# Batch 0's tokens in quarters, a held weight load and paired transposes in an attention and MLP kernel

## The chip, the cores and the metric

The kernel runs on one core of one Trainium2 chip. The metric is device time in microseconds (us) of one execution; the number compared is the median of several runs. Times inside an execution come from the hardware profiler, counted from the start of its span.

## The reference

`x` is (8, 8, 512, 64): batch, head, token, feature. `state` is (8, 8, 32, 64). All inputs are float32.

```
scores  = 1/8 * x @ state^T                # per batch and head: 512 x 32
a       = softmax(scores, over the 32)     # max taken off, 1e-9 added to the sum
xread   = a @ state                        # 512 x 64
scores2 = 1/8 * state @ x^T                # 32 x 512
a2      = softmax(scores2, over the 512)
sread   = a2 @ x                           # 32 x 64
y       = concat([xread, sread], tokens)   # 544 rows per head
rows    = y with the heads side by side    # (8 * 544) x 512
out     = leaky_relu(rows @ w_in, 0.01) @ w_out    # w_in 512 x 2048, w_out 2048 x 512
```

## The kernel before, in words

The instruction order on every engine is written out by hand. The tile pools decide only where buffers lie; waits follow from the data.

**The algebra.** For the 512 token rows of a batch, `xread @ w_in` is computed as `a @ (state @ w_in)`. `a_m` (matmuls on L384) makes a piece of `M = state @ w_in` for one 512-column chunk of w_in, `m_evict` (L396, L398) casts it to SBUF, and `ff1` (L405, for batch 0 `ff1_0` on L632) multiplies it with the transposed probabilities `aT`. `piece` (L433) is the second product with w_out, in four quarters `jq` of the sum for each of four row blocks `i`. The 256 state rows of all batches go through the MLP at the end (`ff1_s`).

**Start.** SP issues the transfers of batch 0's tokens (tiles `xf`), ACT that of the first states (`st0f`). GpSimd (POOL) makes an identity and small masks, and then issues in order the loads of w_in (four chunks of 512 columns, cast to bf16 by the DMA), w_out, batch 1's tokens (`x1`) and batch 2's (`xl`). TensorE (PE) first runs `spin` matmuls on zeros, seven of them, then `state01` (transposed states, tile `stbd`), then three more.

**Batch 0.** Two halves `u` of four heads. `cast_x0` casts tokens to bf16, PE transposes them (`x0_half`, L487), `xt0_evict` copies them from PSUM (L494), `scores0` makes the scores with tokens on the partitions (L502, tiles `sct`), `max0` takes maxima (L531), `split0` splits each into two bf16 parts, `rows0` computes the scores again with states on the partitions (L514), and `spread0` adds the maxima to them by matmuls (L523). `exp0`, `sum0`, `recip0`, `recip0_rows` and `probs0` finish the softmax (L544 to L567). Then come `a_m` of chunks 0 and 1, the first four `ff1_0` blocks, and `a_m` of chunk 2, which needs w_in's third load.

**Batches 2 to 7.** A loop over batches with 16 slots `s`. Every slot holds one `ff1` block of the batch and one `piece`; between them stand steps of the next batches: token load (s = 0), scores and maxima (s = 1), exponentials (s = 5 to 7), `a_m` (s = 10), a DMA transpose of the tokens after next (s = 13).

**Second probabilities.** `a_probs2` writes `a2` (states on the partitions). A DMA transpose from SP makes `a2T`, and `a_sread` (PE L357, ACT copies on L364) reads it for `sread`. Batches 0 and 1, and batches 6 and 7, share a tile `a2p` and are transposed in one DMA (`a_a2t_pair`); batches 2 to 5 have one DMA each (`a_a2t`, L339), issued at s = 0 behind the token load (L99), with `a_sread` at s = 8 of the same batch. `a_sread` of batches 0 and 1 stands at s = 4 and 6 of batch 2, that of batch 6 at s = 6 of batch 7.

Of the kernel before, what the change touches and what calls it, by code (L numbers as in the profile page):

```python
# [9 lines left out]
P = 128  # L10
B, H, S, D = 8, 8, 512, 64
NS = 32
# [3 lines left out]
NT = S // P  # L16
NK = H // 2
SCALE = 1.0 / (D ** 0.5)

BF16 = mybir.dt.bfloat16  # L20
FP32 = mybir.dt.float32
# [6 lines left out]
def kernel(  # L28
# [9 lines left out]
    nc = tc.nc  # L38

    consts = ctx.enter_context(tc.tile_pool(name="consts", bufs=1))  # L40
# [18 lines left out]
    nc.scalar.dma_start(  # L59
        st0f[:], state[0:2].rearrange("b h n d -> (b h n) d").rearrange("(p r) d -> p r d", r=4)  # L60
    )
    xf = [consts.tile([P, NK, 2 * P], FP32, name="xf", tag=f"xf{u}") for u in range(2)]
    xv = x[0].rearrange("h (p t) d -> p h (t d)", t=NT)
    for u in range(2):
        nc.sync.dma_start(xf[u][:], xv[:, NK * u:NK * (u + 1)])

    idle = consts.tile([P, S], BF16, name="idle")
    nc.vector.memset(idle[:], 0.0)
    warm = consts.tile([P, 2], FP32, name="warm")
# [2 lines left out]
    ident = consts.tile([P, P], BF16, name="ident")  # L72
# [47 lines left out]
    def pair_of(a, t, k):  # L120
        h = 2 * (k % 2)
        return a.xb[k // 2][:, t, h:h + 2, :].rearrange("p h d -> p (h d)")
# [11 lines left out]
            xl[b][:].rearrange("p h (t d) -> p h t d", t=NT),  # L134
        )

    def cast_x0(h0, h1, copy):
        u = h0 // NK
        copy(
            xs[0][u][:, :, h0 - NK * u:h1 - NK * u].rearrange("p t h d -> p h t d"),  # L140
            xf[u][:, h0 - NK * u:h1 - NK * u].rearrange("p h (t d) -> p h t d", t=NT),
        )

    def load_w_in(c):
        nc.gpsimd.dma_start(  # L145
            w_in_bf[:, :, DM * c:DM * (c + 1)],
            moe_w_in[:, DM * c:DM * (c + 1)].rearrange("(k p) f -> p k f", p=P),
        )

    def load_w_out(c):  # L150
        nc.gpsimd.dma_start(
            w_out_bf[:, 4 * c:4 * (c + 1), :],
            moe_w_out[DM * c:DM * (c + 1), :].rearrange("(j p) f -> p j f", p=P),
        )

    def spin(n, tag):
        p = psum.tile([P, S], FP32, name="pspin", tag=tag, bufs=2 if tag in ("ph", "py") else 1)
        for _ in range(n):
            nc.tensor.matmul(p[:], lhsT=idle[:, :P], rhs=idle[:], start=True, stop=True)
# [102 lines left out]
    def block_sub(flat, m1, n):  # L262
        m1b = att.tile([P, n, NS], FP32, name="mrowb", tag="mrowb", bufs=1)
        nc.vector.transpose(m1b[:], m1[:, :, None].to_broadcast([P, n, NS]))  # L264
        sh = att.tile([P, n * NS], FP32, name="sh", tag="sh")
        nc.vector.tensor_tensor(  # L266
            out=sh[:], in0=flat, in1=m1b[:].rearrange("p c j -> p (c j)"), op=ALU.subtract,
        )
        return sh
# [51 lines left out]
    def a_probs2(a):  # L321
        nc.vector.tensor_scalar(out=a.r2[:], in0=a.r2[:], scalar1=1e-9, scalar2=None, op0=ALU.add)
        q2 = att.tile([P, 2], FP32, name="qc", tag="qc")
        nc.vector.reciprocal(q2[:], a.r2[:])
        if a.b in (0, 6):
            pairs[a.b] = att.tile([P, 2, 2, S], BF16, name="a2p", tag="a2p", bufs=1)
        if a.b in (0, 1, 6, 7):
            a.a2 = pairs[a.b - a.b % 2][:, a.b % 2]
        else:
            a.a2 = att.tile([P, 2, S], BF16, name="a2", tag="a2", bufs=1)[:]  # L330
        for g in range(2):
            nc.vector.tensor_scalar(
                out=a.a2[:, g, :], in0=a.e2[:, g, :],
                scalar1=q2[:, g:g + 1], scalar2=None, op0=ALU.mult,
            )

    def a_a2t(a):
        t = att.tile([P, 2, NT, P], BF16, name="a2T", tag="a2T", bufs=1)
        nc.sync.dma_start_transpose(  # L339
            t[:].rearrange("p g i q -> p (g i) q"), a.a2.rearrange("p g s -> p (g s)")  # L340
        )
        a.a2T = t[:]

    def a_a2t_pair(b):
        t = att.tile([P, 2, 2, NT, P], BF16, name="a2pT", tag="a2pT", bufs=1)
        nc.sync.dma_start_transpose(
            t[:].rearrange("p b g i q -> p (b g i) q"),
            pairs[b][:].rearrange("p b g s -> p (b g s)"),
        )
        for v in range(2):  # L350
            att_of[b + v].a2T = t[:, v]
# [125 lines left out]
    VEC(stb0[:], st0f[:])  # L477
    spin(7, "py")
    state01()
    spin(3, "py")  # L480

    def x0_half(u):
        pxt = [psum.tile([P, NT, P], BF16, name="pxth", tag=("ph", "py")[u]) for _ in range(2)]
        for v in range(2):
            for t in range(NT):
                h = NK * u + 2 * v
                nc.tensor.transpose(  # L487
                    pxt[v][:, t, :], pair_of(a0, t, h // 2), ident[:]
                )
        return pxt  # L490

    def xt0_evict(u, pxt, copies):
        for v, copy in enumerate(copies):
            copy(a0.xT[:, :, 2 * u + v, :], pxt[v][:])  # L494

    sct = [psum.tile([P, NG, NS], FP32, name="sct", tag=tag, bufs=1) for tag in ("sc", "big")]

    def scores0(u):
        for v in range(2):
            for t in range(NT):  # L500
                c = NK * t + 2 * v
                nc.tensor.matmul(  # L502
                    sct[u][:, c:c + 2, :].rearrange("p c n -> p (c n)"),
                    lhsT=a0.xT[:, t, 2 * u + v, :],
                    rhs=stbd[:, 2 * u + v].rearrange("p g n -> p (g n)"),
                    start=True, stop=True,
                )

    scn, e10, r0, qb0 = {}, {}, {}, {}

# [55 lines left out]
    def probs0(u):  # L566
        nc.vector.tensor_tensor(out=a0.aT[:, u], in0=e10[u][:], in1=qb0[u][:], op=ALU.mult)  # L567

    load_w_in(0)
    load_w_in(1)  # L570
    cast_x0(0, 2, VEC)
    cast_x0(2, 4, SCA)
    pxt = x0_half(0)
    xt0_evict(0, pxt, (VEC, SCA))
    cast_x0(4, 6, VEC)
    for c in range(2, 4):
        load_w_in(c)
    cast_x0(6, 8, POO)
    load_w_out(0)
    x1 = [consts.tile([P, NK, 2 * P], FP32, name="x1", tag=f"x1{u}") for u in range(2)]  # L580
    for u in range(2):
        nc.gpsimd.dma_start(
# [6 lines left out]
    a0.aT = att.tile([P, 2, S], BF16, name="aT", tag="aT")  # L589
    open_xb(1)  # L590
    a_open(a1, 1)
    scores0(0)
    pxt = x0_half(1)
    m = max0(0)
    xt0_evict(1, pxt, (SCA, VEC))
    rows0(0)
    m = split0(m)
    scores0(1)
    m = m, max0(1)
    rows0(1)  # L600
    spread0(scn[0], m[0], False)
# [153 lines left out]
    for b in range(2, B):  # L755
        hT = hpool.tile([P, 16, S], BF16, name="hT", tag="hT")
        a = att_of[b]
        nxt = att_of[b + 1] if b + 1 < B else None
        order = [(b - 1, i, 3) for i in range(2)]
        order += [(b - 1, i, jq) for i in range(2, NT) for jq in range(4)]  # L760
        order += [(b, i, jq) for jq in range(3) for i in range(2)]
        for s in range(16):
            ff1(a, hT, s)
            if s == 0:
                if b + 2 < B:
                    load_x(b + 2, nc.sync)
                    open_xb(b + 2)
                if b == 7:
                    a_a2t_pair(6)
                elif b != 6:  # L770
                    a_a2t(a)
            elif s == 1:
                if nxt is not None:
                    a_scores(nxt)
                m_evict(a, 3, a_m(a, 3, "big"), SCA)
                if nxt is not None:
                    a_shift(nxt)
                    a_max2(nxt)
                if b + 2 < B:
                    cast_all(b + 2)  # L780
            elif s == 4:
                if b == 2:
                    load_state(1)
                    a_sread(a0)
            elif s == 6:
                if b in (2, 7):
                    a_sread(a1 if b == 2 else att_of[6])
            elif s == 8:
                if b != 6:
                    a_sread(a)  # L790
                if b == 2:
                    state_cast(1)
                    state_t(1)
            if nxt is not None:
                if s == 5:
                    a_exp(nxt)
                elif s in (6, 7):
                    a_exp2(nxt, s - 6)
                    if s == 7:
                        a_probs(nxt)  # L800
                        a_probs2(nxt)
                elif s == 10:
                    pm0 = a_m(nxt, 0, "big")
                    pm2 = a_m(nxt, 2, "phpy")
                    pm1 = a_m(nxt, 1, "sc")
                    m_evict(nxt, 2, pm2, VEC)
                    m_evict(nxt, 0, pm0, VEC)
                    m_evict(nxt, 1, pm1, SCA)
                if s == 13 and b + 2 < B:
                    a_open(att_of[b + 2], b + 2)  # L810
                    a_xt_dma(att_of[b + 2])
            pb, i, jq = order[s]
            piece(pb, hT if pb == b else h_prev, i, jq)
        h_prev = hT
# [48 lines left out]
```

## Time and profile before

| | |
|---|---|
| median of 3 runs | 216.64 us (216.63 to 217.03) |
| the profiled execution's own time | 216.83 us |
| its span | 214.4 us |
| PE busy | 207.1 us, 97% of the span |
| ACT / DVE / POOL busy | 137.8 / 99.4 / 23.2 us |
| HBM read / written | 17.30 / 8.91 MB |

Busy times are sums over the span, so 97% says that PE is the engine to look at, not that every microsecond of it is needed: the spin matmuls count as busy too. Some matmul records are missing from the trace, so a gap on PE of about one matmul may be a record that was lost. An engine's wait is put down to the semaphore that came last. A DMA has two times: how long its issue keeps the issuing queue, and how long after the issue the data have landed.

### The profile page before, as it was taken

To read this page: it belongs to the slowest core of one execution; us is meant where nothing else is said; L and a number is where in the kernel's file an instruction comes from. 1 tells how busy PE (TensorE), PEld (TensorE's weight loads), DVE (VectorE), ACT (ScalarE), POOL (GpSimd) and SP (SyncE) were. 2 spreads that over 40 slices of the span, in tenths; PEclk is the share of its full clock that TensorE was granted. 3 is DMA by queue.
4 is the path that set the end of the run, shared out by engine and by line. 5 is a ranking of instruction groups with operands and counts; after the bars stand their busy time and mean duration, and the time that the engine had idled before them with its cause. 6 is when DMAs were issued, how large, how long until landed. Compare 5 with 4: busy or idle time off the path is not lost.

```text
span 214.4 us, 3689 instructions
## 1 busy us (share of the span) xinstructions
PE 207.1 (97%) x1482; PEld 97.4 (45%) x1508; DVE 99.4 (46%) x152; ACT 137.8 (64%) x261; POOL 23.2 (11%) x38
## 2 busy tenths in 40 slices
PE   7889999999999999999999999999999999999993
PEld 2533534344454444444454445444444455466553
DVE  1668598699857246741784096706680000000000
ACT  3468567988788476856696579647774756464420
POOL 8831001030031012000200030000000000000000
PEclk9999999999999999999999999999999999999998
DMA  6999995685994991189217931422124210111123
GB/s 174 226 206 293 208 279 116 165 278 88 222 254 119 141 252 67 52 173 232 84 52 150 228 117 49 101 46 101 49 68 79 73 73 3 49 52 49 49 52 98
DMA packets 39872, 27.70 MB, mean 129 GB/s; under 512 B 24496, under 2 KB 35120, under 8 KB 39856
## 3 DMA queue, kind: packets, MB, share of 16 engines
q1 hardware_dynamic: 34912, 21.04, 39.8%
q0 software_dynamic: 4800, 6.29, 14.5%
q10 hardware_dynamic: 144, 0.13, 0.5%
q8 instruction: 12, 0.20, 0.4%
q14 instruction: 4, 0.03, 0.1%
HBM read 17.30 MB, written 8.91 MB: 122 GB/s over the span
## 4 chain that ended last, share of the span: by engine, by line
PE 87%; DMA 5%; DVE 3%; POOL 2%; issue 1%; ACT 1%; POOLq 0%; ACTq 0%
PE py L433 48%; PE ph L405 21%; DMA w_in_bf<-in_moe_w_in_dram 5%; PE pm L384 4%; PE ph L416 3%; PE pyw L433 3%; PE ph L632 2%; PE psr L357 2%; PE pyh L459 2%; PE sc L246 1%; POOL w_in_bf L145 1%; DVE mrow L256 1%; DVE mrowb L264 1%; DVE M L398 1%; DVE sh L266 1%
## 5 line engine op out<-in xcount | busy, mean ns | idle before, releaser
L433 PE MATMUL py<-w_out_bf,hT 128*128 128x512 bf16 x444 | 116.4, 379 | 1.0
L410 ACT ACTIVATE hT<-ph 128x512 bf16<-128x512 f32 x112 | 66.4, 601 | 40.0 <-PE ph L405 39.4
L433 PEld LDWEIGHTS <-hT 128*128 128x128 bf16 x496 | 46.7, 98 | 57.0 <-issue 5.3
L405 PE MATMUL ph<-aT,M 128*128 128x512 bf16 x223 | 65.3, 379 | 0.2
L405 PEld LDWEIGHTS <-M 128*128 128x128 bf16 x224 | 21.7, 98 | 27.3 <-issue 1.9
L442 ACT COPY ysb<-py 128x512 f32<-128x512 f32 x31 | 18.2, 586 | 10.7 <-PE py L433 10.7
L256 DVE TRANSPOSE_TENSOR_REDUCE mrow<-sc 128x32 f32<-128x1024 f32 x7 | 8.7, 1250 | 32.6 <-PE sc L246 32.6
L464 DVE COPY ysh<-pyh 128x256 f32<-128x256 f32 x1 | 0.4, 424 | 48.2 <-PE pyh L459 48.2
L132 POOL CAST xb<-xl 128x2048 bf16<-128x2048 f32 x5 | 9.5, 1894 | 77.4 <-DMA xl<-in_x_dram 44.7
L398 ACT CAST M<-pm 128x1024 bf16<-128x1024 f32 x13 | 13.2, 1013 | 1.2 <-PE pm L384 0.6
L278 DVE TRANSPOSE_TENSOR_REDUCE r<-e 128x32 f32<-128x1024 bf16 x7 | 8.7, 1242 | 10.1 <-ACT e L273 10.1
L398 DVE CAST M<-pm 128x1024 bf16<-128x1024 f32 x9 | 11.0, 1218 | 1.8 <-PE pm L384 1.8
L314 ACT ACTIVATE e<-sc,mcols 128x512 bf16<-128x512 f32 x16 | 11.2, 701 | 0.3 <-DVE mcols L308 0.3
L396 DVE CAST M<-pm 128x512 bf16<-128x512 f32 x12 | 7.7, 685 | 5.4 <-PE pm L384 5.4
L306 DVE TENSOR_REDUCE mcol<-sc 128x2 f32<-128x1024 f32 x8 | 9.7, 1214 | 0.0
L420 ACT ACTIVATE hs<-ph 128x256 bf16<-128x256 f32 x16 | 6.0, 385 | 4.6 <-PE ph L416 4.4
L287 DVE STREAM_TRANSPOSE qb<-qh 128x1024 bf16<-128x1024 bf16 x7 | 8.7, 1246 | 0.2
L264 DVE STREAM_TRANSPOSE mrowb<-mrow 128x1024 f32<-128x1024 f32 x7 | 8.7, 1245 | 0.2
L266 DVE TENSOR_TENSOR sh<-sc,mrowb 128x1024 f32<-128x1024 f32 x7 | 8.6, 1225 | 0.2
L416 PE MATMUL ph<-sr_t,w_in_bf 128*128 128x256 bf16 x64 | 8.3, 273 | 0.0
L640 ACT ACTIVATE hT<-ph 128x512 bf16<-128x512 f32 x12 | 6.4, 597 | 2.4 <-PE ph L632 2.1
L273 ACT ACTIVATE e<-sh 128x1024 bf16<-128x1024 f32 x7 | 7.3, 1050 | 0.6 <-DVE sh L266 0.6
(98 smaller groups left out, 155.0 us busy)
## 6 DMA issues: line engine op xcount, KB each, us to landing
out_dram<-ysb SPq DMA_DIRECT2D x31, 256.0 KB, 2.4
xl<-in_x_dram SPq DMA_DIRECT2D x5, 1024.0 KB, 7.3
w_in_bf<-in_moe_w_in_dram POOLq DMA_DIRECT2D x4, 512.0 KB, 9.4
w_out_bf<-in_moe_w_out_dram POOLq DMA_DIRECT2D x4, 512.0 KB, 16.7
xf<-in_x_dram SPq DMA_DIRECT2D x2, 512.0 KB, 5.1
x<-in_x_dram POOLq DMA_DIRECT2D x2, 512.0 KB, 13.6
xl<-in_x_dram POOLq DMA_DIRECT2D x2, 512.0 KB, 17.1
out_dram<-ysb SPq DMA_DIRECT2D x8, 64.0 KB, 1.7
```

Of the source, the lines that this page charges most:

```text
L132: nc.gpsimd.tensor_copy(xt[b][:].rearrange("p t h d -> p h t d"), xl[b][:].rearrange("p h (t d) -> p h t d", t=NT),)
L256: nc.vector.tensor_reduce(out=m1[:], in_=flat.rearrange("p (c j) -> p c j", j=NS), axis=AX.X, op=ALU.max, apply_transpose=True,)
L264: nc.vector.transpose(m1b[:], m1[:, :, None].to_broadcast([P, n, NS]))
L266: nc.vector.tensor_tensor(out=sh[:], in0=flat, in1=m1b[:].rearrange("p c j -> p (c j)"), op=ALU.subtract,)
L306: nc.vector.tensor_reduce(out=m2[:], in_=a.sc[:], axis=AX.X, op=ALU.max, negate=True)
L314: nc.scalar.activation(out=a.e2[:, g], in_=a.sc[:, g, :], func=AF.Exp, bias=a.m2s[:, g:g + 1], scale=SCALE, accum_out=a.r2[:, g:g + 1],)
L398: copy(a.M[:, :, cols], pm[:])
L405: nc.tensor.matmul(ph[:], lhsT=a.M[:, g, P * j:P * (j + 1)], rhs=a.aT[:, g, :], start=(g == 0), stop=(g == 1),)
L410: nc.scalar.activation(out=hT[:, j, :], in_=ph[:], func=AF.Prelu, alpha=0.01)
L416: nc.tensor.matmul(ph[:, :n], lhsT=w_in_bf[:, k, P * j:P * (j + 1)], rhs=sr_t[:, k, :], start=(k == 0), stop=(k == NK - 1),)
L433: nc.tensor.matmul(y.py, lhsT=hT[:, j, P * i:P * (i + 1)], rhs=w_out_bf[:, j, :], start=(j == 0), stop=(j == 15),)
L442: copy(ysb[:], ys[b, i].py)
```

## The change

- Batch 0's tokens come in four transfers of two heads each, in place of two of four heads. The casts go by quarters: the first on GpSimd, the other three on VectorE (before: VectorE, ScalarE, VectorE, GpSimd).
- GpSimd sets a tile `held` (128 x 640 bf16) to zero before it issues w_in's first load. Its cast of quarter 0 stands between w_in's first and second loads.
- Transposes, copies and scores go by quarters. Three quarters are transposed before any is scored; ScalarE copies the first three, VectorE the last, ahead of the first maximum. The three `spin` matmuls after `state01` are gone.
- Second probabilities of batches (2, 3) and (4, 5) are transposed in pairs too, at s = 0 of the odd batch. `a_sread` of an even batch moves to s = 6 of the batch after it. `a2p` gets two buffers, `sh` one in place of two.

```diff
-    for u in range(2):
-        nc.sync.dma_start(xf[u][:], xv[:, NK * u:NK * (u + 1)])
+    for q in range(NK):
+        nc.sync.dma_start(xf[q][:], xv[:, 2 * q:2 * q + 2])
+    held = consts.tile([P, 640], BF16, name="held")
...
-        sh = att.tile([P, n * NS], FP32, name="sh", tag="sh")
+        sh = att.tile([P, n * NS], FP32, name="sh", tag="sh", bufs=1)
...
-        if a.b in (0, 6):
-            pairs[a.b] = att.tile([P, 2, 2, S], BF16, name="a2p", tag="a2p", bufs=1)
-        if a.b in (0, 1, 6, 7):
-            a.a2 = pairs[a.b - a.b % 2][:, a.b % 2]
-        else:
-            a.a2 = att.tile([P, 2, S], BF16, name="a2", tag="a2", bufs=1)[:]
+        if a.b % 2 == 0:
+            pairs[a.b] = att.tile([P, 2, 2, S], BF16, name="a2p", tag="a2p")
+        a.a2 = pairs[a.b - a.b % 2][:, a.b % 2]
...
     state01()
-    spin(3, "py")
+    def x0_t(q):
+        ps = psum.tile([P, NT, P], BF16, name="pxth", tag=("ph", "py")[q // 2])
+        for t in range(NT):
+            nc.tensor.transpose(ps[:, t, :], pair_of(a0, t, q), ident[:])
+        return ps
...
+    nc.gpsimd.memset(held[:], 0.0)
     load_w_in(0)
-    load_w_in(1)
-    cast_x0(0, 2, VEC)
-    cast_x0(2, 4, SCA)
-    pxt = x0_half(0)
-    xt0_evict(0, pxt, (VEC, SCA))
-    cast_x0(4, 6, VEC)
-    for c in range(2, 4):
+    cast_x0(0, POO)
+    for q in range(1, NK):
+        cast_x0(q, VEC)
+    for c in range(1, 4):
         load_w_in(c)
-    cast_x0(6, 8, POO)
     load_w_out(0)
+    pxt = [x0_t(q) for q in range(3)]
+    for q, copy in ((0, SCA), (1, SCA), (2, SCA)):
+        xt0_evict(q, pxt[q], copy)
+    for q in range(2):
+        scores0(q)
+    xt0_evict(3, x0_t(3), VEC)
...
-    scores0(0)
-    pxt = x0_half(1)
     m = max0(0)
-    xt0_evict(1, pxt, (SCA, VEC))
     rows0(0)
     m = split0(m)
-    scores0(1)
+    for q in (2, 3):
+        scores0(q)
...
-                if b == 7:
-                    a_a2t_pair(6)
-                elif b != 6:
-                    a_a2t(a)
+                if b % 2:
+                    a_a2t_pair(b - 1)
...
             elif s == 6:
-                if b in (2, 7):
-                    a_sread(a1 if b == 2 else att_of[6])
+                if b == 2 or b % 2:
+                    a_sread(att_of[b - 1])
             elif s == 8:
-                if b != 6:
+                if b % 2:
                     a_sread(a)
```

More of the change, by code (lines that the diff above doesn't have):

```diff
@@ L61 @@
     )
-    xf = [consts.tile([P, NK, 2 * P], FP32, name="xf", tag=f"xf{u}") for u in range(2)]
+    xf = [consts.tile([P, 2, 2 * P], FP32, name="xf", tag=f"xf{q}") for q in range(NK)]
     xv = x[0].rearrange("h (p t) d -> p h (t d)", t=NT)
-    for u in range(2):
-        nc.sync.dma_start(xf[u][:], xv[:, NK * u:NK * (u + 1)])
+    for q in range(NK):
+        nc.sync.dma_start(xf[q][:], xv[:, 2 * q:2 * q + 2])
+    held = consts.tile([P, 640], BF16, name="held")
     idle = consts.tile([P, S], BF16, name="idle")
@@ L135, in cast_all, with cast_x0 @@
         )
-    def cast_x0(h0, h1, copy):
-        u = h0 // NK
+    def cast_x0(q, copy):
+        v = q % 2
         copy(
-            xs[0][u][:, :, h0 - NK * u:h1 - NK * u].rearrange("p t h d -> p h t d"),
-            xf[u][:, h0 - NK * u:h1 - NK * u].rearrange("p h (t d) -> p h t d", t=NT),
+            xs[0][q // 2][:, :, 2 * v:2 * v + 2].rearrange("p t h d -> p h t d"),
+            xf[q][:].rearrange("p h (t d) -> p h t d", t=NT),
         )
@@ L335, in a_probs2 @@
             )
[L337 to L342, printed above, removed]
     def a_a2t_pair(b):
@@ L479, with xt0_evict, scores0 @@
     state01()
-    spin(3, "py")
[L482 to L494, printed above, removed]
-    sct = [psum.tile([P, NG, NS], FP32, name="sct", tag=tag, bufs=1) for tag in ("sc", "big")]
[L498 to L507, printed above, removed]
+    def x0_t(q):
[3 more added lines that the diff above has]
+        return ps
+    def xt0_evict(q, ps, copy):
+        copy(a0.xT[:, :, q, :], ps[:])
+    sct = [psum.tile([P, NG, NS], FP32, name="sct", tag=tag, bufs=1) for tag in ("sc", "big")]
+    def scores0(q):
+        for t in range(NT):
+            c = NK * t + 2 * (q % 2)
+            nc.tensor.matmul(
+                sct[q // 2][:, c:c + 2, :].rearrange("p c n -> p (c n)"),
+                lhsT=a0.xT[:, t, q, :], rhs=stbd[:, q].rearrange("p g n -> p (g n)"),
+                start=True, stop=True,
+            )
     scn, e10, r0, qb0 = {}, {}, {}, {}
```

## The prediction

> **What bounds the kernel now.** I read the page first, then PE's waits, the chain of waits, the timeline of the first 32 us and the stretches of the DMA queues. The page:
>
> ```profile
> span 214.4 us, 3689 instructions
> PE 207.1 (97%) x1482; PEld 97.4 (45%) x1508; DVE 99.4 (46%) x152; ACT 137.8 (64%) x261; POOL 23.2 (11%) x38
> ...
> PEclk9999999999999999999999999999999999999998
> DMA  6999995685994991189217931422124210111123
> ```
>
> TensorE is the bound, and the DMA engines are full over the first six slices (32 us). PE's waits from 15.3 us to the end:
>
> ```profile
> PE pm L384 <- DMA w_in_bf<-in_moe_w_in_dram: 0.2, 1, 0.2
> ```
>
> That is the whole list, and it is the wait that has just ended at 15.23. From there on PE never idles long enough to be listed: gaps of one matmul's length (0.43 us between starts where 0.216 is usual) are missing records, 1482 matmuls against 1508 weight loads. So only what happens before 15.23, or a new stall, can move the end. What sets 15.23 is in the chain of waits (start, length, what) and in the timeline:
>
> ```profile
> 4.50 10.69 DMA w_in_bf<-in_moe_w_in_dram
> 15.23 0.63 PE pm L384 x16
> ```
>
> ```profile
> 6.98 0.79 POOL L139 CAST xb<-xf 128x512 bf16<-128x512 f32 x1 [0.87 <-DMA xf<-in_x_dram]
> ...
> 7.50 0.69 DVE L531 TENSOR_REDUCE m<-sct 128x16 f32<-128x512 f32 x1 [0.20 <-PE sct L502]
> ...
> 8.26 0.42 DVE L494 COPY xT<-pxth 128x512 bf16<-128x512 bf16 x1
> ...
> 9.07 0.69 DVE L531 TENSOR_REDUCE m<-sct 128x16 f32<-128x512 f32 x1
> ...
> 13.09 0.39 PE L632 MATMUL ph<-aT,M 128*128 128x512 bf16 x1
> ...
> 15.23 0.41 PE L384 MATMUL pm<-w_in_bf,stbd 64*32 64x512 bf16 x8 [0.24 <-DMA w_in_bf<-in_moe_w_in_dram]
> ```
>
> Two paths meet at 15.23: batch 0's attention, which lets PE begin real work at 13.09 and reaches this point with 0.24 us to spare, and the third chunk of w_in, which lands at 4.50 + 10.69 = 15.19. The second path ends last. It meets PE again later: of the waits up to 45 us,
>
> ```profile
> PEld L246 <- DMA st_t<-stb: 0.5, 1, 0.5
> ```
>
> is batch 2's scores at 40.15, waiting for a transposed state that landed at 36.94 + 3.2 = 40.1 (PE itself loses 0.05: 0.14 between starts where 0.09 is usual). That hangs on batch 2's tokens, loaded behind all the weights (issued 15.47, landed 17.6 later). The DMA path thus holds PE at two places, and the change takes no bytes off it. The stretches of the DMA queues (last column GB/s):
>
> ```profile
> 5.50:6.00 0.50, 0.33 (x4) 0.13 (x4) 0.32 (x1) 0.50 (x1) 0.50 (x1) 1.00 1.10 344
> 6.00:6.25 0.25, 0.25 (x7) 0.25 (x6) 0.00 (x0) 0.00 (x1) 0.12 (x1) 1.00 1.22 250
> ...
> 7.00:8.00 1.00, 0.84 (x14) 0.58 (x12) 0.80 (x2) 0.33 (x2) 1.00 (x2) 1.00 1.22 204
> ```
>
> Batch 0's tokens move at 340 to 390 GB/s from 3.0 to about 6.1, then the casting w_in loads at 204 (bytes written), with no gap. w_in's first load, issued at 2.84, moves next to nothing before 6.0.
>
> **The change part by part.**
>
> *Four transfers.* The halves landed at 0.75 + 4.6 = 5.36 and 1.27 + 5.6 = 6.85, 1.49 apart: 0.745 a quarter, so quarters at 4.6, 5.35, 6.1 and 6.85. Two more SP issues (0.47 each) end near 2.6, ahead of any need. The last may land up to 0.3 earlier if w_in no longer shares 6.0 to 6.5, or no earlier; I take 6.85, since the stream before it is already full.
>
> *The hold.* POOL's memsets took 0.20 us for 128 and 0.26 for 196 columns, 0.9 ns a column; 640 columns give about 0.65 (0.5 by a slope of 0.6 from the 32-row memsets). w_in's first issue moves from 2.84 to 3.45. If its data were ready and queued when x0 ended, this costs nothing; if the 3.1 us from issue to first data (2.84 to about 6.0) are all latency, data start at 6.6 and the queue stands still for 0.45. Nearest rows: 64 KB stores landed 1.7 us after issue in all, and the state loads issued at 23.89 into a full queue took 4.5; so most of a long delay is queueing. I take 0 and keep 0.45. The other three w_in loads move behind the POOL cast, from 3.72 to about 5.5; w_in's first load lands at 9.31, which covers them by some 3 us. Token and weight loads behind them issue 0.3 later (7.72 to 8.0) and wait in the queue until 17.63 anyway.
>
> On sharing, the Trainium skill ("DMA: Bandwidth & Descriptors", Queues, rings and completion order) says that a DMA engine alternates between the queues that have work, packet by packet. By that rule w_in would slow x0 as soon as it is ready and the hold would win that time back; this trace shows x0 at 344 GB/s up to 6.0, so there is little to win back, and by the rule the sum below would be at most 0.3 lower on the attention path, which is not the path that ends last.
>
> *Batch 0's chain.* Quarter 0: POOL cast 0.79 from 4.7 (POOL started 0.13 after landing at 6.98) to 5.5; four transposes to the copy's start 0.49 (cast end 5.82 to copy 6.31): 6.0; three ACT copies of 0.59: 6.6, 7.2, 7.75. Scores of quarter 1 at 7.2; then quarter 3's transposes, whose DVE cast (0.43 from 6.87) is done at 7.30; DVE copy 7.8 to 8.2. Here DVE is in order, so the first maximum, which ran at 7.50 while DVE waited for POOL's cast, now stands behind that copy: 8.2 to 8.9, split 0.4 to 9.3 (8.97 before), second maximum 0.69 to 10.0 (9.76), split to 10.4 (10.18). So the chain gets 0.2 longer: it loses POOL's 0.79 for DVE's 0.43, and gains one 0.69 maximum in series. Real work starts at 13.3, and PE comes to the w_in wait at 15.2 instead of 14.99. The 0.24 of cover just hides it: between 0 and 0.05 on the end, 0.1 to 0.4 if copies or POOL run later than counted. The dropped three spin matmuls (4.76 to 5.70) freed nothing that was waited for.
>
> *Pairs.* Batches 2 and 4 lose their own transposes (SP busy 3.2 and 2.5 us), 3 and 5 issue double ones behind a 1 MB token load, and batch 2's and 4's state reads (16 matmuls, 0.47 us, two ACT copies of 0.26) move into slot 6 of the next batch. PE's work is the same. Cover for the doubled transpose in batch 3: issued at 73.1, the single one landed 7.5 later at 80.6, 0.9 after its token load (72.42 + 7.3); twice the blocks add about 0.9: 81.5. The read now starts two slots before the old one (87.53 less 2 x 1.295 = 84.94): 3.4 to spare. In batch 5: 125.1 against 130.4. The upper bound, twice 7.5 from issue, gives 88.1 and a 3.2 stall. ACT's two copies beside the exponentials are what batch 2 already has at slots 4, 6 and 8, where PE shows no wait. One buffer for sh: its reader is done at 31.83, its next writer starts near 43. SP's stores wait up to 0.8 longer behind the longer issue, with four output buffers to cover. All of this: 0.
>
> *Sum.* The profiled execution took 216.83 (214.4 span and 2.43 around it), 0.19 over the median. Quarters and hold 0, chain +0.2 of which 0.04 to 0.05 passes the w_in wait, pairs 0: 216.9 for such an execution, 216.7 against the median.
>
> **The rivals.**
>
> *The hold starves the queue (0.15).* If w_in's first data come 3.1 us after issue whatever the queue, all landings slip 0.45, with both DMA waits of PE: 217.1. It decides once the hold exceeds the time that w_in's descriptors lay ready before 6.1. For it: data started just as x0 ended. Against it: the 1.7 us of small stores.
>
> *TensorE's clock falls back (0.10).* The first seven spins took 3.17 us, 0.45 each, the next three 0.94, later 512-column matmuls 0.216: the array doubles its speed near 5.0, although the granted clock reads 1.00 throughout. Without the three spins PE works, by the timeline's rows, an estimated 1.5 of the 3.4 us after 4.9 (before: 2.3). If that lets it fall back, the spreads, rows, sums and products between 5.5 and 13.1 take twice their time, some 1.5 us on the path, of which the cover takes 0.04: 218.1. Against it: at 50% busy from 10.3 to 13.1 it stays fast. The Trainium skill ("TensorE: Matmul & The Clock Gate", The HAM clock gate) has the clock halved after an idle window of about 3.4 us; by that rule the scattered work would hold it, unless transposes don't count as work, as its part on PE-mode transposes says. No run here shows which.
>
> *A chain or transpose longer than counted (0.11).* ACT's serial copies or w_in slipping ahead of quarter 3 add 0.5 to 0.8: 217.3; a stalled state read (0.03 of it) up to 220.
>
> *Faster (0.12).* w_in's landings are 2.51, 3.37 and 2.44 apart; were the third even, all later loads would land 0.87 sooner and both DMA waits vanish. With quarter 3 landing 0.3 sooner and scores hidden as they land, the chain could be 0.3 shorter: 0.24 + 0.3 gives 216.1.
>
> **How the numbers follow.** The forecast case has 0.52 and runs from 216.3 to 217.05. Within 0.2% (0.43 us, about what a measurement of this kernel can tell) is that case: 0.52. Slower is the first three rivals, 0.36; faster 0.12. The range reaches to the third rival and takes part of the faster one: 216.2 to 217.7, leaving out the clock and the far ends.
>
> **What would show it.** Right: quarters landing near 4.6, 5.4, 6.1, 6.85; the first ff1 matmul (L632's line) near 13.3; the a_m matmuls behind it still at 15.2 to 15.3, released by w_in; PE without waits in batches 3 and 5. Wrong: a stretch near 6.3 with low GB/s and w_in's third chunk past 15.5 (first rival); 512-column matmuls 0.4 apart between 9 and 13 (second); the wait before a_m gone and PE there before 15.0 (faster).

## The result and the profile after

The changed kernel took 218.24 us in the median of six executions (217.40 to 219.30), the kernel before 216.79 beside it (216.63 to 217.03): a ratio of 1.0072, 95% interval [1.0055, 1.0089]. It is slower, and its median lies above the predicted range. Its profiled execution is its shortest, 217.40 with a span of 215.3, so what follows here explains 0.9 us of span and no more; the rest needs the experiments. The six spans are 215.3 to 216.3; of what lies outside the span (2.10 to 2.16 us in four of the six) two executions have 0.7 and 0.9 us more, and no profile shows what that is. All ratios leave out the two executions that were over 1.5% slower than the fastest of their kernel (220.22 of the quarters alone, 220.81 with w_in's second load ahead of the cast).

The page of the changed kernel:

```profile
span 215.3 us, 3679 instructions
...
PE 206.2 (96%) x1479; PEld 97.2 (45%) x1505; DVE 99.2 (46%) x152; ACT 137.9 (64%) x261; POOL 23.6 (11%) x39
...
PEclk9999999999999999999999999999999999999999
DMA  6999994775884992184217931332024110111113
```

PE is busy for 0.9 us less because the three spin matmuls that are gone took 0.94; the span is 0.9 longer because PE waits. PE's waits from 15.3 us to the end (total, times, longest):

```profile
PE pm L375 <- DMA w_in_bf<-in_moe_w_in_dram: 1.1, 1, 1.1
PE py L424 <- issue: 0.3, 2, 0.2
PE ph L396 <- ACT hT L401: 0.2, 1, 0.2
```

The first is the wait that was 0.2 before; the second are two gaps of 0.16 us for which the profile shows no other engine; the third is taken up with the pairs. The chain of waits shows what set it, and the timeline where batch 0's attention stood (start, length, what):

```profile
2.95 0.64 POOL held L553
3.59 0.82 POOL w_in_bf L146
4.41 0.00 issue
4.41 0.62 POOL xb L140
5.03 0.80 POOL w_in_bf L146
5.83 10.05 DMA w_in_bf<-in_moe_w_in_dram
```

```profile
12.96 0.39 PE L617 MATMUL ph<-aT,M 128*128 128x512 bf16 x1
...
15.93 0.41 PE L375 MATMUL pm<-w_in_bf,stbd 64*32 64x512 bf16 x8 [1.07 <-DMA w_in_bf<-in_moe_w_in_dram]
```

The chain now runs through the memset of `held` and the cast on GpSimd into the third w_in load, which lands at 5.83 + 10.05, at 15.89, instead of 15.19. The attention chain is 0.13 earlier than before (first `ff1_0` matmul 12.96, not 13.09) and buys nothing. The stretches of the DMA queues (last column GB/s):

```profile
5.50:6.00 0.50, 0.45 (x5) 0.23 (x4) 0.17 (x2) 0.41 (x1) 0.50 (x2) 1.00 0.96 184
6.00:6.25 0.25, 0.00 (x0) 0.00 (x0) 0.25 (x1) 0.25 (x2) 0.25 (x1) 1.00 1.01 127
...
7.00:8.00 1.00, 0.99 (x15) 0.57 (x15) 0.55 (x2) 0.36 (x1) 1.00 (x2) 1.00 1.23 194
```

Before, the same stretches moved 344, 250 and 204. The tokens end sooner, and w_in does not follow at its rate: behind the tokens the queues move less (127 GB/s).

**Reading all profiles with one rule.** A point that every profile has is ACT's sixth copy of batch 0's hidden layer (L627 in the changed kernel). In the fifteen profiles of the experiments, and in the two of before and after, it starts at the later of two times: w_in's third landing + 2.54, or the first `ff1_0` matmul + 4.33, to within 0.02 us. So each kernel's front is read from two numbers, and each loss is put to the weights or to the attention chain.

| profile of | w_in's third chunk lands | first `ff1_0` matmul | sixth copy | set by |
|---|---|---|---|---|
| before | 15.19 | 13.09 | 17.73 | w_in |
| changed | 15.89 | 12.96 | 18.43 | w_in |
| changed, again | 16.43 | 14.27 | 18.97 | w_in |
| hold doubled | 17.33 | 15.19 | 19.87 | w_in |
| changed front, pairs undone | 15.65 | 13.99 | 18.32 | chain |
| before, quarters only | 16.70 | 16.89 | 21.21 | chain |
| before, without the three spins | 14.87 | 15.37 | 19.70 | chain |
| changed, without the hold | 15.07 | 16.40 | 20.72 | chain |

From here to PE's last matmul the profiles differ by another -0.3 to +0.5, nearly all of it before 53 us (batch 2's state and first copies).

### The profile page after: what moved, and what is told of

The parts are those of the page before. It is cut to its first block, busy times and chain, and to the rows that moved or that the text cites. A ratio compares the mean times of both kernels' runs of the same rounds, so it can differ in the third digit from the quotient of the medians.

```text
span 215.3 us, 3679 instructions
## 1 busy us (share of the span) xinstructions
PE 206.2 (96%) x1479; PEld 97.2 (45%) x1505; DVE 99.2 (46%) x152; ACT 137.9 (64%) x261; POOL 23.6 (11%) x39
## 4 chain that ended last, share of the span: by engine, by line
PE 85%; DMA 5%; DVE 3%; POOL 2%; issue 1%; ACT 1%; SPq 1%; POOLq 0%; ACTq 0%
PE py L424 49%; PE ph L396 21%; DMA w_in_bf<-in_moe_w_in_dram 5%; PE pm L375 4%; PE ph L407 3%; PE pyw L424 3%; PE ph L617 2%; PE psr L348 2%; PE sc L247 1%; POOL w_in_bf L146 1%; DMA out_dram<-ysb 1%; DVE mrow L257 1%; DVE mrowb L265 1%; DVE mcols L309 1%; DVE M L389 1%
## 5 line engine op out<-in xcount | busy, mean ns | idle before, releaser
L396 PE MATMUL ph<-aT,M 128*128 128x512 bf16 x219 | 64.5, 379 | 0.3 <-ACT hT L401 0.2
L375 PE MATMUL pm<-w_in_bf,st_t 64*32 64x512 bf16 x192 | 7.6, 379 | 0.1
```

The lines of the kernel that those rows point to most:

```text
L375: nc.tensor.matmul(at[v][NS * r:NS * (r + 1)], lhsT=st_of(a, g, k), rhs=w_in_bf[D * g:D * (g + 1), k, DM * c:DM * (c + 1)], start=True, st ...
L396: nc.tensor.matmul(ph[:], lhsT=a.M[:, g, P * j:P * (j + 1)], rhs=a.aT[:, g, :], start=(g == 0), stop=(g == 1),)
```

## The experiments

The ratios are to the kernel before, measured beside each on the same chip, with 95% intervals; medians of before were 216.74 to 216.82.

### The parts by themselves: hold out, pairs alone, hold alone, front alone

The changed kernel without the memset:

```diff
-    nc.gpsimd.memset(held[:], 0.0)
     load_w_in(0)
```

> The changed kernel without the memset of the held tile; all else as changed. Theory H (the hold, together with tokens that now start 0.38 us sooner, lets the DMA queue run thin between 5.7 and 6.5 us): w_in's first load is issued at 2.84 again, its third lands 0.6 to 1.0 us sooner than the 15.89 of the changed kernel, near 15.0, PE's wait before that product falls from 1.07 to under 0.3 us, and the median comes to 216.3 to 216.8, at or below the kernel before. Rival O (the queue runs thin because w_in's second to fourth loads wait behind GpSimd's cast): the third still lands at 15.6 or later and the median stays above 217.2. Rival P (the paired transposes cost most of it): less than 0.3 us gained, median above 217.7.

Measured: 216.86 (216.59 to 219.46), ratio 1.0012 [0.9991, 1.0034]. Taking out one memset brings the median back to that of before, so in this kernel the median's loss goes with the hold. The third chunk lands at 15.07, as theory H expected; the third load is issued at 5.81, as late as in the changed kernel (5.83), so its place behind the cast (rival O) is not what delays it there. But the profile is from the longest execution, 219.46, and shows the other side. w_in's first data came at 5.25, into the tokens' last quarter, which landed at 8.51 instead of 6.51. PE waited 2.5 us for casts, and from 8.2 to 15.0 the granted clock read 0.50: 128-column matmuls took 0.31 each instead of 0.22, and `ff1_0` began at 16.40.

The kernel before with only the second probabilities in pairs (`a2p`, `a_a2t_pair` and `a_sread` as in the change, `sh` with one buffer):

```diff
-                if b == 7:
-                    a_a2t_pair(6)
-                elif b != 6:
-                    a_a2t(a)
+                if b % 2:
+                    a_a2t_pair(b - 1)
```

> The kernel before with only the paired second probabilities (the tiles' buffers, the pair transposes in batches 3 and 5, the moved state reads). Theory H: no change, 216.6 to 217.0, PE without waits in batches 3 and 5. Rival P: 0.6 to 1.4 us slower than before, with PE waits after 48 us.

Measured: 217.19 (216.66 to 217.64), ratio 1.0014 [1.0004, 1.0024], 0.2 above the range of theory H and below that of rival P. PE's waits from 15 us to the end in this kernel:

```profile
PE py L423 <- issue: 0.3, 2, 0.2
PE ph L395 <- ACT hT L400: 0.3, 1, 0.3
PE pm L374 <- DMA w_in_bf<-in_moe_w_in_dram: 0.2, 1, 0.2
```

None of it is a wait for a transposed tile. From ACT's 29th to its 124th copy of the hidden layer (52 to 185 us) this kernel takes 133.63 us, the kernel before 133.63, the changed one 133.64. The 0.3 on `hT` stands near 48 us, where ACT's exponentials waited 0.50 for `mcols` instead of 0.28. It is not the pairs' own: the changed kernel has it in its first profile (0.2 above) and not in its second, and two kernels without the pairs have it (0.2 with three token transfers, 0.7 with four on two queues). So the pairs cost nothing in the steady state; where the 0.1 to 0.5 us of the ratio lie, this profile does not show.

The kernel before with only a hold (two memsets of 300 columns, which move the first issue from 2.84 to 3.65):

```diff
+    held = consts.tile([P, 300], BF16, name="held")
+    for _ in range(2):
+        nc.gpsimd.memset(held[:], 0.0)
     load_w_in(0)
     load_w_in(1)
```

> The kernel before with two memsets of 300 columns ahead of w_in's first load (0.6 us of hold), tokens still in halves. Theory H: in the changed kernel the data came 2.1 us after the issue, so here they are ready near 5.6, before the halves end at 6.15: 0 to 0.2 us slower than before. If the 3.1 us from issue to data in the kernel before were all latency: 0.5 to 0.6 us slower, data from 6.6.

Measured: 217.19 (216.77 to 217.42), ratio 1.0013 [1.0004, 1.0023]. The third chunk landed at 15.48, 0.29 later, and PE ended 0.15 later. With w_in's loads issued in one go behind the hold, the 0.8 us by which they are issued later cost 0.3 at the landing and, by the ratio, 0.1 to 0.5 in time; half a microsecond is hidden.

The changed kernel with its pairs undone (front, hold and `sh` as changed):

```diff
-                if b % 2:
-                    a_a2t_pair(b - 1)
+                if b == 7:
+                    a_a2t_pair(6)
+                elif b != 6:
+                    a_a2t(a)
```

> The changed kernel with the second probabilities of batches 2 to 5 transposed singly as before (sh keeps one buffer). Theory H: as the changed kernel, 217.4 to 218.5, third w_in load near 15.9. Rival P: back to within 0.3 us of the kernel before.

Measured: 218.15 (217.41 to 219.12), ratio 1.0060 [1.0038, 1.0082]: the loss is in the front. In this profile w_in's third chunk lands at 15.65, yet it is the chain that sets the end, with `ff1_0` at 13.99. The reason is TensorE: up to 10.5 us its 128-column matmuls took 0.31, then 0.22, and the granted clock read 1.00 all along. By the rule the weights alone would have set 18.19 in place of 18.32, so the slow array costs this execution 0.13.

### A second profile, the loads' order, the length of the hold, the quarters alone

The changed kernel again, unaltered:

> The changed kernel once more, unaltered, for a second profile: the first one came from its fastest execution (span 215.3), while its median is 0.8 us above that. Theory W (w_in comes late: the hold and the later issues leave the DMA queues thin behind batch 0's tokens, so all landings slip and PE waits for w_in's third chunk): 217.9 to 218.5, the wait before the a_m matmuls (L375) 1.0 or more, w_in's third chunk at 15.9 or later, first ff1 matmul near 13. Theory T (the attention chain is late: w_in's packets get between those of the last quarters on a few DMA engines, in some executions more than in others): the same time, but the last quarter lands after 6.7, first ff1 matmul after 13.5, and the wait before a_m is under 0.5 or gone.

Measured: 219.22 (218.00 to 220.01), ratio 1.0108 [1.0083, 1.0133]; the profile is of an execution of 218.78 with a span of 215.6, so 1.1 us more than in the first profile lies outside the span. TensorE was fast here and the tokens landed at 4.46, 5.23, 5.97, 6.64. But w_in's first three chunks landed at 11.35, 13.89 and 16.43 (9.81, 12.34, 15.89 in the first profile), and PE waited 0.98 for the second and 0.30 for the third. Theory W holds for this execution's front; the one thing theory T names that is there, a late `ff1_0`, came from w_in's second chunk.

w_in's second load ahead of the cast on GpSimd:

```diff
     load_w_in(0)
+    load_w_in(1)
     cast_x0(0, POO)
-    for c in range(1, 4):
+    for c in range(2, 4):
         load_w_in(c)
```

> The changed kernel with w_in's second load issued ahead of POOL's cast, as in the kernel before; the hold and everything else stay. Theory W in the form that the second load is what is missing (only one load's packets are ready when the tokens end at about 5.8 to 6.0): 216.8 to 217.3, stretch from 6.0 to 6.5 above 200 GB/s instead of 127 and 147. Theory W in the form that the first load's own delay counts: 217.8 to 218.5 as the changed kernel, since the first data still come near 5.7. Theory T: as the changed kernel or up to 0.5 more, since more w_in packets stand beside the last quarter; POOL's cast of quarter 0 about 0.3 later as well.

Measured: 217.96 (216.77 to 220.81), ratio 1.0044 [1.0027, 1.0061]. The median is in the range of W's second form; the profile lies between the two forms: the third chunk lands at 15.53, 0.36 sooner than in the changed kernel, and 6.0 to 6.5 moved 180 GB/s. It is again set by the chain (`ff1_0` at 14.23), with a granted clock of 0.50 from 7.8 to 11.2 us.

The hold twice:

```diff
-    nc.gpsimd.memset(held[:], 0.0)
+    for _ in range(2):
+        nc.gpsimd.memset(held[:], 0.0)
```

> The changed kernel with the memset of held twice (1.28 us of hold instead of 0.64); nothing else differs. Theory W: every landing 0.5 to 0.65 later, w_in's third chunk near 16.5, the wait before a_m 1.6 to 1.8, time 218.6 to 219.1. Theory T: the tokens are then undisturbed in every execution, quarters at 4.3, 5.1, 5.8, 6.5 and ff1 at 12.9, so the slow executions go: spread under 0.5 between executions and 217.6 to 218.2 in the median. If the hold were hidden by the queue (my forecast): as the changed kernel, 218.2.

Measured: 219.06 (217.80 to 220.44), ratio 1.0109 [1.0077, 1.0140]. The third chunk lands at 17.33 and the execution follows it. The landing is 1.44 later than the changed kernel's for 0.64 more of hold, more than a shift. Stretches of this kernel:

```profile
6.00:6.50 0.50, 0.50 (x7) 0.50 (x6) 0.50 (x2) 0.07 (x1) 0.50 (x2) 1.00 0.48 80
...
9.00:10.00 1.00, 1.00 (x24) 0.61 (x26) 0.93 (x4) 0.00 (x0) 1.00 (x2) 1.00 0.82 96
```

At 9 us three w_in loads and more were issued (the third's issue ended at 7.35), and the DMA engines still moved half of the usual 205. The packet records show single 1 KB packets of w_in that take 0.2 to 1.5 us where nearly all take 0.098. Counted up to 12 us there are none over 0.2 in the kernel before, 27 and 29 in the two profiles of the changed kernel, 39 here, 9 with the hold alone; over all runs, 13 to 36 with the full hold and the changed front, 5 with half the hold, 0 to 12 without a hold. So they are more frequent with the full hold and the changed front; what holds up such a packet, the records don't say.

The quarters alone, in the kernel before:

```diff
-    xf = [consts.tile([P, NK, 2 * P], FP32, name="xf", tag=f"xf{u}") for u in range(2)]
+    xf = [consts.tile([P, 2, 2 * P], FP32, name="xf", tag=f"xf{q}") for q in range(NK)]
-    for u in range(2):
-        nc.sync.dma_start(xf[u][:], xv[:, NK * u:NK * (u + 1)])
+    for q in range(NK):
+        nc.sync.dma_start(xf[q][:], xv[:, 2 * q:2 * q + 2])
```

> The kernel before with only its two token transfers cut into four (its casts of two heads each then wait for a quarter, not a half); no hold, w_in's order, the spins and the pairs as before. Theory W: 216.5 to 217.0, no loss, since w_in's issues stay at 2.84 to 5.2 and only the chain gets earlier, behind a wait for w_in that stays at 15.2. Theory T: more transfers on SP's queue and their tails cost by themselves: 217.2 or more, last quarter past 6.9 and ff1 past 13.3.

Measured: 217.57 (216.86 to 220.22), ratio 1.0054 [1.0026, 1.0082]. Seven executions lie at 216.86 to 217.61 and five at 218.64 to 220.22, these five with a mean clock of 0.989 to 0.992. The profile is from the longest, 220.22; 219.70 and 219.88 are alike in clock. Its chain of waits, and its stretches:

```profile
2.27 7.22 DMA xf<-in_x_dram
9.50 0.02 issue
...
9.63 0.62 POOL xb L139
```

```profile
10.00:12.00 2.00, 1.70 (x20) 0.91 (x24) 0.95 (x4) 0.00 (x0) 2.00 (x4) 0.69 1.24 205
12.00:14.00 2.00, 1.64 (x41) 0.94 (x34) 0.77 (x3) 0.60 (x1) 1.95 (x3) 0.50 1.24 206
```

The fourth transfer, issued at 2.27, landed 7.22 later. Between 6.5 and 9.5 us the tokens' queue started its last 12 packets of 1 KB while w_in started 566. PE then idles from 7.5 to 10.3 and its clock falls to half at 10.8. The signs of theory T are all here: a median above 217.2, the last quarter past 6.9, `ff1_0` past 13.3.

### The spin matmuls and the hold

The changed kernel with the three spins after `state01` back:

```diff
     state01()
+    spin(3, "py")
```

> The changed kernel with the three spin matmuls after the state's transposes put back; hold, quarters and pairs stay. The profiles so far give the time of ACT's sixth copy of batch 0's hidden layer as the later of w_in's third landing + 2.54 and first ff1 matmul + 4.33. Theory C (without the three spins TensorE misses its faster clock in some executions, which makes ff1 1.0 to 1.3 late): ff1 at 12.9 to 13.2, copies of four transposes 0.40 or less from 6.3 on, w_in alone sets the time (third chunk 15.6 to 16.4): 217.5 to 218.3, spread between executions under 1.2, no clock under 0.995. Theory W alone (w_in's landings are the whole loss, the spins do nothing): as the changed kernel, 218.2 to 219.2 with executions up to 220.

Measured: 217.78 (217.30 to 219.32), ratio 1.0068 [1.0044, 1.0092]. The median is in theory C's range, and the time is set by w_in (third chunk at 16.10), but the spread did not shrink to its bound, `ff1_0` came at 13.94, and the ratio is not clear of the changed kernel's two (1.0072 and 1.0108, intervals from 1.0055 to 1.0133). The timeline says why; first the same line of before, then this kernel:

```profile
4.76 0.94 PE L159 MATMUL pspin<-idle 128*128 128x512 bf16 x3
```

```profile
4.76 1.46 PE L160 MATMUL pspin<-idle 128*128 128x512 bf16 x3
6.01 1.36 PE L476 MATMUL pxth<-ident,xb 128*128 128x128 bf16 x12
```

The array doubled its speed at 5.0 in the one execution and only at 7.1 in the other, so that quarter 0's transposes, ready at 5.1, stood behind slow spins until 6.0.

Spins back and hold gone:

```diff
     state01()
+    spin(3, "py")
...
-    nc.gpsimd.memset(held[:], 0.0)
     load_w_in(0)
```

> The changed kernel with the three spins back and the hold gone (w_in's first load again issued near 2.84). Theory C with W: w_in's third chunk at 15.0 to 15.3 and ff1 at 12.9 to 13.2, so 216.5 to 216.9, as the kernel before or 0.2 less; single executions 1 to 2.5 above it where w_in's packets delay the last quarter past 8 (then the clock reads under 0.993). If the four transfers cost by themselves: 217.2 or more in the median.

Measured: 217.37 (216.62 to 219.72), ratio 1.0041 [1.0017, 1.0065]. Five of twelve executions are within 217.0, but the median is in the range set for four transfers that cost by themselves; two with clocks of 0.990 and 0.992 are at 218.6 and 219.7. In its profile `ff1_0` is at 13.23 and the third chunk at 15.57.

Only the three spins taken out of the kernel before:

```diff
     state01()
-    spin(3, "py")
```

> The kernel before with only its three spin matmuls after the state's transposes taken out. Theory C: in some executions TensorE stays at half speed up to about 10 us, where the first four transposes take 0.5 to 0.6 instead of 0.4, and ff1 slips by 1.0 to 1.3, of which 0.24 is covered: the executions fall in two groups, one at 216.6 to 217.0 and one at 217.5 to 218.2. Theory W alone: no difference, 216.6 to 217.0 in all.

Measured: 217.94 (217.15 to 219.05), ratio 1.0061 [1.0038, 1.0084]; all nine executions but one are above the longest of before (217.19). This settles that in the kernel before the spins carry something, though the executions don't fall in the two groups expected. Its timeline:

```profile
6.29 1.03 PE L486 MATMUL pxth<-ident,xb 128*128 128x128 bf16 x8 [1.08 <-DVE xb L139]
...
10.67 0.32 PE L522 MATMUL scn<-ident,hi 128*32 128x128 bf16 x4
...
12.67 0.23 PE L522 MATMUL scn<-ident,hi 128*32 128x128 bf16 x4
```

Eight transposes take 1.03 instead of 0.62, the spreads of the first half 0.32 instead of 0.23, those of the second half 0.23: the array reached its speed at 12.4. `ff1_0` slips to 15.37, 2.28 later, of which the tokens in this execution explain 0.2 (landed 5.58 and 7.02).

Spins back, half the hold:

```diff
-    held = consts.tile([P, 640], BF16, name="held")
+    held = consts.tile([P, 320], BF16, name="held")
...
     state01()
+    spin(3, "py")
```

> The changed kernel with the three spins back and the hold cut in half (a memset of 320 columns, about 0.33 us). With the two runs with spins and the full or no hold this is a series in the hold alone. Theory W (the loss grows with the hold): between the two, 217.0 to 217.6, w_in's third chunk 15.3 to 15.7. If w_in's data were ready well before the tokens end, as I forecast: as without a hold, 216.5 to 216.9.

Measured: 217.98 (216.93 to 219.26), ratio 1.0062 [1.0040, 1.0084]. Its ratio lies between those of full and no hold, its median above both. The profile is of its shortest execution: third chunk at 14.79, `ff1_0` at 13.90 behind three spins of 1.46 us as above. As a series in the hold alone the three are inconclusive: their intervals overlap, and with the spins in a varying place the chain sets the time as often as w_in.

### Does the last transfer's time of issue count?

Three transfers in the kernel before (two quarters and a half, issued by 2.23):

```diff
-    for u in range(2):
-        nc.sync.dma_start(xf[u][:], xv[:, NK * u:NK * (u + 1)])
+    for u, (h, n) in enumerate(((0, 2), (2, 2), (4, 4))):
+        nc.sync.dma_start(xf[u][:], xv[:, h:h + n])
```

> The kernel before with batch 0's tokens in three transfers (two quarters and the second half), all issued by 2.25 instead of 2.75; w_in's first issue stays at 2.84. Theory I (a transfer issued just ahead of w_in's first one loses packets to w_in's, so it is the time of the last issue that counts): the last transfer lands by 6.9 in every execution, no clock under 0.995, 216.5 to 217.0, as the kernel before. Theory N (the number of transfers or their smaller pieces cost by themselves): between two and four transfers, 217.0 to 217.4 in the median with single executions of 218.5 to 220.

Four transfers in the kernel before, on two queues (issued by 2.18):

```diff
-        nc.sync.dma_start(xf[q][:], xv[:, 2 * q:2 * q + 2])
+        (nc.sync, nc.scalar)[q % 2].dma_start(xf[q][:], xv[:, 2 * q:2 * q + 2])
```

> The kernel before with only the four token transfers, as in the run of quarters alone, but the second and fourth issued on ACT's queue, so that all four are issued by about 2.1 instead of 2.75. Theory I: as the kernel before, 216.5 to 217.0, the last quarter landing by 7.0 and no clock under 0.995. Theory N: as the quarters on one queue, 217.4 to 217.8 with 4 to 5 of 12 executions above 218.5.

The changed front without hold, with spins, on two queues (both edits above in the changed kernel):

> The changed kernel without its hold, with the three spins back, and with the tokens' second and fourth transfer on ACT's queue: the version that keeps the changed kernel's front and drops the two costs found. Theory I: w_in's third chunk at 14.9 to 15.3, ff1 at 13.0 to 13.5, every execution between 216.4 and 217.1, so at best as the kernel before and never slower. Theory N: 217.2 to 217.6 with executions above 218.5, as with one queue.

Measured, in this order: 217.16 (216.82 to 218.45), ratio 1.0024 [1.0011, 1.0037]; 217.50 (217.05 to 218.66), ratio 1.0033 [1.0021, 1.0046]; 217.52 (216.80 to 218.70), ratio 1.0038 [1.0024, 1.0052]. In 34 executions no clock is under 0.997, where quarters on one queue had 5 of 12 at 0.992 or less, and the profiles have the last transfer at 6.67 to 6.73. So the long tails and the clock's fall go with the last transfer being issued at 2.27, just ahead of w_in's first load at 2.84; that half of theory I holds. That four transfers on one queue are enough for a tail is not ruled out by these runs alone, but the six profiles with the full or the doubled hold have four on one queue, w_in's first load 1.25 us or more behind the last, and the last quarter at 6.51 to 6.81. The other half of theory I, that the time then equals that of before, does not hold: 0.4 to 0.8 us remain, and all three medians lie in the ranges of theory N (of its executions above 218.5 there is one in each run with two queues). With three transfers PE is even done 0.11 us sooner than before and the last store landed 0.10 sooner (213.40 against 213.50), while the span ends 0.3 later: what the profile doesn't explain is after the work. With two queues quarter 1 shares the DMA engines with quarter 0 and lands at 5.65 to 5.69 instead of 5.0 to 5.4, and `ff1_0` is 0.1 to 0.4 later than before; in the kernel before with two queues PE then waits 0.7 near 48 us, which makes most of its later end. No version tried beats the kernel before.

## Why the prediction was wrong

- **What bounds the front: right.** Two paths meet at the third `a_m`, and the rule behind its sum (landing or chain, whichever is later) reproduces the meeting point in all profiles. The bound was read well; the terms put into it were not.
- **The step that failed first: the hold at 0 (kept: 0.45).** The memset took 0.64 (estimated 0.65) and the first issue moved to 3.52 (3.45). Then the prediction argued that w_in's data would lie ready in a full queue when the tokens end, because small stores land 1.7 us after issue. Much of the delay was queueing (first data 3.1 us after issue before, 1.6 with the hold doubled), and here the first data were there in time, at 5.66, 2.1 us after issue. But there were not enough of them: as the tokens ran out at 6.05, w_in moved 127 GB/s, and its first chunk landed 0.50 later than before. Third landings were 0.34 to 1.24 later in the five profiles with the full hold and the changed front (15.53 to 16.43). The upper bound was too small as well, since it counted a shift; slow packets came on top. The rival "the hold starves the queue", at 0.15, had the mechanism and a third of the price: 0.45, where the median rose by 1.4.
- **The step that failed second: "the dropped three spin matmuls freed nothing that was waited for".** True of the queue, false of the array. In the kernel before, their removal alone costs 1.2 us in the median. Of the seven profiles without them the array sped up by 5.3 us in four, and only at 10.5 (pairs undone), 10.0 (hold doubled) and 12.4 us (spins out) in three; with them it was fast by 7.1 in all ten. The clock rival had 0.10 and its price, 1.5 us, was about right, but its mechanism was a fall back from full speed. That is what three other profiles show (hold out, second load earlier, quarters alone); in the three late ones the array had not yet got there, and that "the granted clock reads 1.00 throughout" hid it (see the last section). The Trainium skill ("TensorE: Matmul & The Clock Gate", The HAM clock gate) says that the rate doubles after a busy window of about 3.4 us and that the window runs freely. The trace agrees: in each of the 17 profiles all changes of the clock lie whole multiples of 3.41 us apart, and the place of these stretches differs between executions. Without the spins PE's first run of work, from 1.2 us on, ends near 5, so it hangs on where the stretch lies whether one is full enough (last section). What this costs the changed kernel itself is not shown: putting the spins back gained nothing clear with the hold (1.0068) nor without it (1.0041 against 1.0012), and with the spins and the hold both out ten of twelve executions were no longer than the longest of before beside them (217.40).
- **Four transfers: right in spacing, wrong in tail.** Quarters landed at 4.33, 5.08, 5.83 and 6.51, 0.75, 0.75 and 0.68 apart (predicted 0.745), 0.27 to 0.34 ahead of the forecast. That the last could be late by 3 us was priced at 0.5 to 0.8 under a rival. On sharing, which the prediction weighed by the Trainium skill ("DMA: Bandwidth & Descriptors", Queues, rings and completion order), the trace of the quarters alone leaves turns between the queues open. The last five token packets started 0.13 us apart, as turns with w_in's packets of 0.098 on one engine might give; from 6.91 to 8.06 no token packet started at all. Which engine each packet ran on, and whether the tokens' descriptors were there to be served, no record shows.
- **Batch 0's chain: near.** Forecast 0.2 longer, measured 0.13 shorter where the array was fast, because the quarters came sooner; the maxima did go in series behind DVE's copy.
- **Pairs: right at 0** in the steady state, within 0.01 us over 133.6; alone in the kernel before they measured 0.1 to 0.5 us, and the cause is not found.
- **The range.** It left out the clock with 0.10 and cut the hold at 0.45. Both were bounds that no row of the trace set: the trace of before had w_in's first load issued at 2.84 and a full run of spins, and so showed neither cost.

How the median comes to 1.4 us is not a sum of the parts: the later landing and the missing speed are each there in some executions, and only the later path counts; a tail of the tokens is in no profile with the full or the doubled hold. Open remain what stalls w_in's packets after a hold, how the loss divides between hold and spins in the changed kernel, and the time after the last store.

## What to carry to other kernels

Where two paths meet closely, find the rule that gives the meeting point from both and read every variant with it; a part that helps the earlier path is worth nothing, and a delay on the later one moves the meeting point in full. Spin matmuls that nobody waits for may still be holding the array's clock: price their removal by the work behind them at half speed. Take several profiles of a kernel that spreads: the shortest execution showed a third of the causes.

## What was not expected of the hardware

- The granted clock read 1.00 while TensorE worked at half speed from its start (0.31 instead of 0.22 us for a 128-column matmul); after a fall behind idle time it read 0.50. The row reads 1.00 where the trace holds no clock record: the first record begins between 3.94 us (quarters alone) and 12.41 us (spins out), and in every profile that is where the matmuls become shorter. So a mean clock of 1.00 does not exclude a slow start; the length of one matmul tells.
- Cut into the stretches of 3.41 us that the clock's changes mark, the 17 profiles agree. The array sped up only behind stretches in which PE's records show it busy for 80% or more, and stayed slow behind those of 80% or less. It fell back behind three, with 18, 44 and 57%, and kept its speed behind all of 63% or more.
- The tokens' last transfer, issued at 2.27, 0.57 us ahead of w_in's first load, landed 6.2 and 7.2 us after its issue in two profiles; with w_in's load held, or in other executions, the same 256 KB took 4.2 to 4.5. Issued at 1.69 or 1.77, a last transfer showed no such tail.
- w_in's first data came 1.6 to 3.1 us after the start of the issue, the tokens' 1.4 to 2.4, the states' 1.07 in nearly every profile.
